# Turning the keys of 13 units in place of 9 with VectorE and GpSimd, and scaling both output halves with one multiply

## The chip, the cores and the metric

The kernel runs on one core of a Trainium2 chip. The metric is device microseconds of one execution, without the host. Each kernel ran several times; medians and ranges are given, and states are compared only among "fast" runs, as all profiled runs here were. Four engines matter: TensorE (PE in the profile; PEld is its weight load), ScalarE (ACT), VectorE (DVE) and GpSimd (POOL). SyncE (SP) issues the DMAs.

## The reference, cut to what matters

```python
B, Sq, D = 8, 32, 1024;  Hq, Hkv, Sk, Dh = 32, 4, 8192, 128
W = min(4096, max(256, Sk // 4))                  # 2048: the last 2048 keys
q = (x @ wq).reshape(B, Sq, Hq, Dh)               # to (B, Hq, Sq, Dh)
k, v = the last W rows of k_cache, v_cache, each of the 4 heads used by 8 query heads
p = softmax(q @ k^T * Dh**-0.5)
out = (p @ v, back to (B, Sq, Hq * Dh)) @ wo
```

There are 32 units, one for each pair of batch entry and key head: 256 queries against 2048 keys. All in bfloat16.

## The kernel before: the parts that matter

The score matmuls of this kernel take K with the 128 features on the partitions, but memory holds keys by rows. So K of each unit is turned, in one of three ways: units 0 to 4 by TensorE transposes, most others by a transposing DMA, and the units listed in `V_T` by VectorE and GpSimd. In the last way VectorE transposes each 32x32 block where it stands, into a second buffer (4 instructions of 0.685 us each, "blocks"), and then 16 copies of 32 partitions each ("moves", 0.672 us each on GpSimd) put the blocks where they belong. The fifth number of a `V_T` entry says how many of the 16 moves GpSimd takes; VectorE takes the others.

```python
V_T = {5: (2, (5, 6, 8, 10), 10, 17, 12),         # load with unit 2, blocks in these slots, moves from slot 10 to 17, 12 moves on GpSimd
       **{u: (u - 4, range(4 * u - 16, 4 * u - 12), 4 * u - 13, 4 * u - 4, 16) for u in (8, 11, 14, 17, 20, 23, 26, 29)}}
...
self.krp = pool("krp", 4)      # raw K, rows as in memory
self.kbp = pool("kbp", 2)      # K with its blocks turned
self.kvt = pool("kvt", 2)      # kTv: K turned by VectorE and GpSimd
...
        def move(k, d):
            ...
            if d >= V_T[ui][4] // 4:
                nc.vector.tensor_copy(out=out, in_=in_)
            else:
                nc.gpsimd.tensor_scalar(out=out, in0=in_, scalar1=1.0, scalar2=1.0, op0=ALU.mult, op1=ALU.mult)
```

The main loop has four slots to a unit, 128 in all, numbered through. In a slot TensorE computes scores (`s_ps`) for 512 keys, ScalarE their exponentials, and TensorE the product with V (`o_ps`) of two slots earlier. V goes through a VectorE copy (`va`), because a column of ones beside it gives the softmax's sums.

```python
        for ui, (b, g) in enumerate(self.units):
            ...
            if ui:
                self.va_copy(ui)                  # VectorE
            for c in range(NCH):                  # 4 slots
                for u in loads.get(ui * NCH + c, []):
                    self.load_unit(u)             # SyncE
                ... s_ps matmuls, exponential ...
                while len(pv_queue) > 2:
                    pv_queue.pop(0)()             # o_ps matmuls of two slots ago; at a unit's last one: finish_unit
                ...
                for p in plan[ui * NCH + c]:      # pieces of q and output projections, blocks, moves
                    p()
```

`finish_unit` takes the reciprocal of the sums, scales the unit's output in two halves and turns it for the output projection. At the very end a value is read from memory: all engines branch on it, over a slow fallback path, to the last piece of the program.

## Time and profile before

| | before |
|---|---|
| time, median of the 4 runs beside the changed kernel | 186.84 us (186.51 to 187.57) |
| span of the profiled run | 184.6 us |
| TensorE busy | 180.7 us, 98% |
| VectorE busy, GpSimd busy | 115.1 us, 95.0 us |
| waits of TensorE after the start-up | two of its weight loads, 0.4 and 0.2 us, both at the very end |

The page of the kernel before: its busy time by engine, its chain of waits by engine, and two of its groups (busy time, mean nanoseconds of one, idle time before).

```profile
span 184.6 us, 5057 instructions
...
PE 180.7 (98%) x2057; PEld 154.0 (83%) x2057; DVE 115.1 (62%) x266; ACT 131.7 (71%) x133; POOL 95.0 (51%) x150
...
PE 93%; DMA 4%; SPq 1%; issue 0%; DVE 0%
...
L261 POOL TENSOR_SCALAR kTv<-kb 32x512 bf16<-32x512 bf16 x140 | 94.1, 672 | 64.9 <-PE s_ps L468 38.3
...
L421 DVE TENSOR_SCALAR o_sb<-o_ps,RL_all 128x128 bf16<-128x128 f32 x64 | 19.5, 347 | 1.1
```

The list of waits, for TensorE's matmuls alone, has only these two lines, both from the start-up (total us, number, longest):

```profile
PE warm_ps L346 <- PEq L641: 0.8, 1, 0.8
PE q_ps L376 <- DMA wq_sb<-in_wq_dram: 0.3, 1, 0.3
```

So TensorE bounds the kernel, and between the start-up and the last 8 us nothing makes it wait.

### The profile page before, as it was taken

The page shows a single profiled execution, that of the slowest core. Times are in us where ns is not written, and L with a number is a line of the kernel's source. Part 1 is how long each engine was busy: PE and PEld are TensorE (multiplying, and loading weights), DVE is VectorE, ACT ScalarE, POOL GpSimd, SP SyncE. Part 2 cuts the span into 40 slices and gives each one's busy share as a digit, 9 for nine tenths or more (in the row PEclk, how much of TensorE's full clock was granted, in tenths as well). Part 3 has the DMA queues.
Part 4 walks back from the last instruction along what each step waited for, and adds up shares of the span by engine and source line. Part 5 has one row for each costly group of instructions (what it writes and reads, how often), then busy time and mean ns, then how long its engine had stood idle before and what let it go on. Part 6 is the DMA issues. An engine that isn't in the chain of part 4 may idle for free.

```text
span 184.6 us, 5057 instructions
## 1 busy us (share of the span) xinstructions
PE 180.7 (98%) x2057; PEld 154.0 (83%) x2057; DVE 115.1 (62%) x266; ACT 131.7 (71%) x133; POOL 95.0 (51%) x150
## 2 busy tenths in 40 slices
PE   8999999999999999999999999999999999999994
PEld 2789999999999999988788899988787888888843
DVE  0119799994586686586468549656754865265363
ACT  2207899787789777787878677887776888888800
POOL 2000007949939959928954990797199379700000
PEclk9999999999999999999999999999999999999999
DMA  5999999999999999999999999999999999993003
GB/s 161 283 390 407 408 396 395 260 182 380 262 355 208 389 250 240 340 321 302 233 396 251 303 378 308 240 249 409 301 301 342 260 275 313 282 269 47 0 30 94
DMA packets 52954, 51.73 MB, mean 280 GB/s; under 512 B 39744, under 2 KB 40256, under 8 KB 52928
## 3 DMA queue, kind: packets, MB, share of 16 engines
q1 hardware_dynamic: 52352, 50.90, 99.0%
q10 hardware_dynamic: 576, 0.49, 0.8%
q8 instruction: 16, 0.26, 0.6%
q14 instruction: 10, 0.08, 0.2%
HBM read 41.42 MB, written 0.52 MB: 227 GB/s over the span
## 4 chain that ended last, share of the span: by engine, by line
PE 93%; DMA 4%; SPq 1%; issue 0%; DVE 0%
PE o_ps L479 31%; PE s_ps L468 30%; PE op_ps L295 15%; PE q_ps L275 11%; DMA wq_sb<-in_wq_dram 4%; PE q_ps L376 2%; PE tp L236 2%; SPq L164 1%; PE kf_ps L369 1%; SPq L320 0%; DVE o_t L305 0%; PE cnt_ps L533 0%
## 5 line engine op out<-in xcount | busy, mean ns | idle before, releaser
L470 ACT ACTIVATE pT<-s_ps 128x1024 bf16<-128x1024 f32 x128 | 128.8, 1025 | 32.5 <-PE s_ps L468 31.5
L261 POOL TENSOR_SCALAR kTv<-kb 32x512 bf16<-32x512 bf16 x140 | 94.1, 672 | 64.9 <-PE s_ps L468 38.3
L479 PEld LDWEIGHTS <-pT 128*128 128x128 bf16 x1024 | 68.5, 98 | 3.1
L468 PEld LDWEIGHTS <-kT 128*128 128x128 bf16 x368 | 34.8, 98 | 10.3
L295 PE MATMUL op_ps<-wo_sb,OT 128*128 128x512 bf16 (+2 forms) x144 | 36.2, 355 | 0.0
L275 PE MATMUL q_ps<-xT,wq_sb 128*128 128x256 bf16 x192 | 28.2, 273 | 0.0
L479 PE MATMUL o_ps<-va_112,pT 128*128 128x129 bf16 x352 | 27.1, 220 | 0.0
L479 PE MATMUL o_ps<-va_113,pT 128*128 128x129 bf16 x352 | 27.0, 220 | 0.0
L479 PE MATMUL o_ps<-va_114,pT 128*128 128x129 bf16 x320 | 24.7, 220 | 0.0
L251 DVE STREAM_TRANSPOSE kb<-k_raw 128x512 bf16<-128x512 bf16 x36 | 23.8, 685 | 1.2 <-DMA k_raw<-in_k_cache_dram 1.2
L416 DVE RECIPROCAL RL_all<-o_ps 128x2 f32<-128x2 f32 x32 | 5.3, 164 | 25.8 <-PE o_ps L479 25.7
L421 DVE TENSOR_SCALAR o_sb<-o_ps,RL_all 128x128 bf16<-128x128 f32 x64 | 19.5, 347 | 1.1
L468 PEld LDWEIGHTS <-kTv 128*128 128x128 bf16 x144 | 13.9, 98 | 5.1
L275 PEld LDWEIGHTS <-wq_sb 128*128 128x128 bf16 x192 | 17.0, 98 | 1.2
L468 PE MATMUL s_ps<-QT_63,kT 128*128 128x256 bf16 x112 | 16.8, 272 | 0.0
L423 DVE STREAM_TRANSPOSE OT<-o_sb 128x256 bf16<-128x256 bf16 x32 | 14.2, 445 | 1.1
L468 PE MATMUL s_ps<-QT_66,kT 128*128 128x256 bf16 x96 | 14.4, 273 | 0.0
L295 PEld LDWEIGHTS <-OT 128*128 128x128 bf16 x144 | 11.4, 98 | 2.3 <-DVE OT L423 0.2
L468 PE MATMUL s_ps<-QT_65,kT 128*128 128x256 bf16 x80 | 12.0, 273 | 0.0
L468 PE MATMUL s_ps<-QT_64,kT 128*128 128x256 bf16 x80 | 12.0, 272 | 0.0
L302 DVE TENSOR_TENSOR oacc<-op_ps,oacc 128x512 f32<-128x512 f32 x8 | 5.5, 682 | 7.4 <-PE op_ps L295 7.4
L410 DVE COPY va_113<-v_sb 128x2048 bf16<-128x2048 bf16 x11 | 9.8, 888 | 0.0
(44 smaller groups left out, 105.6 us busy)
## 6 DMA issues: line engine op xcount, KB each, us to landing
v_sb<-in_v_cache_dram SPq DMA_DIRECT2D x30, 512.0 KB, 7.6
wo_sb<-in_wo_dram SPq DMA_DIRECT2D x16, 512.0 KB, 6.9
wq_sb<-in_wq_dram SPq DMA_DIRECT2D x13, 512.0 KB, 7.5
k_raw<-in_k_cache_dram SPq DMA_DIRECT2D x13, 512.0 KB, 6.4
wq_sb<-in_wq_dram SPq DMA_DIRECT2D x6, 256.0 KB, 6.5
v_sb<-in_v_cache_dram SPq DMA_DIRECT2D x4, 256.0 KB, 4.9
kT<-in_k_cache_dram SPq DMA_TRANSPOSE x36, 7.3
k_raw<-in_k_cache_dram SPq DMA_DIRECT2D x2, 256.0 KB, 7.6
```

Of the source, the lines that this page charges most:

```text
L251: nc.vector.transpose(out=st["kb"][:, sl, :], in_=self.k_raw[ui][:, sl, :])
L261: nc.gpsimd.tensor_scalar(out=out, in0=in_, scalar1=1.0, scalar2=1.0, op0=ALU.mult, op1=ALU.mult)
L275: nc.tensor.matmul(st["ps"][:, 0:self.NQ], lhsT=self.wq_t[g, i][:, c % (DC // 2), hl * P:(hl + 1) * P], rhs=self.xT[:, c, :], start=(c == ...
L295: nc.tensor.matmul(ps[:, 0:w], lhsT=self.OT[:, gq, c, t * P:(t + 1) * P], rhs=self.wo_t[gq][:, c, n0:n0 + w], start=(k == 0), stop=(k == 7))
L302: nc.vector.tensor_tensor(out=acc, in0=ps[:, 0:w], in1=acc, op=ALU.add)
L410: self.nc.vector.tensor_copy(out=self.va[ui % 3][:, :, 0:self.Dh], in_=self.v_sb[ui][:, :, :])
L416: nc.vector.reciprocal(out=rl[:, ui * QT_N:(ui + 1) * QT_N], in_=o_ps[:, :, Dh])
L421: nc.vector.tensor_scalar(out=o_sb[:, qt, :, :], in0=o_ps[:, qt, 0:Dh].rearrange("p (i c) -> p c i", c=4), scalar1=rl[:, ui * QT_N + qt:ui ...
L423: nc.vector.transpose(out=self.OT[:, g * QT_N:(g + 1) * QT_N, :, b * self.Sq:(b + 1) * self.Sq], in_=o_sb[:, :, :, :])
L468: nc.tensor.matmul(s_ps[:, jj, :], lhsT=self.kT[ui][:, c * CJ + jj, :], rhs=q_u, start=True, stop=True)
L470: nc.scalar.activation(out=pT[:, :, :], in_=s_ps[:, :, :], func=ACT.Exp, bias=0.0, scale=self.scale)
L479: nc.tensor.matmul(o_ps[:, qt, 0:self.VW], lhsT=pT[:, jj, qt * P:(qt + 1) * P], rhs=va[:, j, 0:self.VW], start=(j == 0 and qt == 0), stop= ...
```

## The change

The intent: take more units away from the transposing DMA (14 in place of 18 are left to it), pay for it with VectorE and GpSimd, which had room, and win some VectorE time back by scaling both halves of a unit's output in one instruction.

```diff
 V_T = {5: (2, (5, 6, 8, 10), 10, 17, 12),
-       **{u: (u - 4, range(4 * u - 16, 4 * u - 12), 4 * u - 13, 4 * u - 4, 16) for u in (8, 11, 14, 17, 20, 23, 26, 29)}}
+       **{u: (u - 4, range(4 * u - 13, 4 * u - 9), 4 * u - 10, 4 * u - 2, 12) for u in range(7, 30, 2)}}
...
-        for qt in range(QT_N):
-            nc.vector.tensor_scalar(out=o_sb[:, qt, :, :], in0=o_ps[:, qt, 0:Dh].rearrange("p (i c) -> p c i", c=4),
-                                    scalar1=rl[:, ui * QT_N + qt:ui * QT_N + qt + 1], scalar2=None, op0=ALU.mult)
+        nc.vector.tensor_tensor(out=o_sb[:, :, :, :], in0=o_ps[:, :, 0:Dh].rearrange("p q (i c) -> p q c i", c=4),
+                                in1=rl[:, ui * QT_N:(ui + 1) * QT_N].unsqueeze(2).unsqueeze(3).to_broadcast([P, QT_N, 4, 32]), op=ALU.mult)
```

## The prediction

> **What bounds the kernel now.** TensorE. The page gives PE 98% of a 184.6 us span at a granted clock of 0.9 or more in every slice; the windows show no gap from 12 us to 176 us. The list of waits gives PE only 1.1 us of waiting, all in the start. The chain that ended last is 93% PE: o_ps 31%, s_ps 30%, op_ps 15%, q_ps 11%. There 8 o_ps matmuls advance in 0.45 us and 4 s_ps matmuls in 0.46 us throughout: no hidden waiting. Everything else has room: ACT 71%, VectorE 115.1 us (62%), GpSimd 95.0 us (51%). DMA is nearly always busy (share 1.1 and over in the windows) but runs ahead.
>
> **What the change does, from the groups of the trace.**
> - DMA: 18 units' K by DMA transpose become 14, so 36 transposing issues become 28; 4 plain K loads more, same bytes. PE doesn't wait for it: gain about 0.
> - VectorE blocks: 16 more at 685 ns, +11 us.
> - VectorE moves: 52 in place of 4, at 449 ns, +21.6 us.
> - GpSimd moves: 156 in place of 140, at 672 ns, +10.8 us (to about 106 us).
> - Multiply: two ops spanning 0.61 us become one of 256 elements per partition. [...]
> Net VectorE: about +26 us, to 141 us (76%); 85 to 93% where the work falls.
>
> **Contention.** [...] GpSimd moves have a median of 611 ns but a longest of 1167; the same va copy takes 0.65 us or up to 1.12. [...]
>
> **How much is critical.** Almost nothing. By unit pair (8 slots, 9.7 to 11.5 us of PE): VectorE needs 4 blocks 2.5, 4 moves 1.9, 2 va copies 1.7, [...] casts and sums 1 to 1.6, so 9 to 9.8 us. GpSimd needs 12 moves at about 0.74 us start to start, 8.9 us, with ten slots until the scores want them. The in-order VectorE queue will lag 1 to 1.5 us at worst, but a va copy has two slots of slack, PSUM tiles two, o_ps five. So I expect PE still without waits, or a few short ones (tightest: slots 31 to 38, where PE needs only 0.92 us a slot). [...]
>
> **Prediction: 187.0 us, range 186.2 to 188.9.** Faster by over 2%: 0.02; within 2%: 0.88; slower by over 2%: 0.10.
>
> **What would show it.** Right: PE still about 181 us busy with no waits of note; VectorE about 140 us; GpSimd 104 to 110 us; fewer SyncE waits and higher GB/s[...]. Wrong: PE waiting for va copies, kTv moves or PSUM copies; GpSimd moves averaging over 750 ns.
>
> **What would make it wrong.** [...] the multiply slower with a stride-zero operand; K loads blocked behind the four raw buffers early on. No step can give 2%, as PE's work is untouched.

Where a cut is marked, an explanation or a figure is gone that no trace or run of this case shows. VectorE's net came to +26 us, to 141 us; of its terms +11 us and +21.6 us still stand, and the term for the multiply is cut: how long the one instruction takes was not measured when this was written. The kernel after and e3 measure it: 0.424 us. The 9 to 9.8 us of VectorE for a unit pair hold the two finishes (the kernel after has 0.17 + 0.42 + 0.45 us for one). The 187.0 us had counted almost nothing as critical.

## More of the kernel before

In the stretch from 36 to 60 us, the windows show (busy time and number of instructions of PE, PEld, DVE, ACT, POOL):

```profile
36.00:60.00 24.00, 24.00 (x298) 22.46 (x296) 16.94 (x44) 19.63 (x21) 16.96 (x26) 1.00 1.15 280
```

## The result, and the profile after

The changed kernel took 193.06 us (median of 4 runs, 192.38 to 194.03), against 186.84 us of the kernel before: ratio 1.035, with an interval of 1.0299 to 1.0402. A ratio here and below is the mean time of one kernel's fast runs over the mean of the other's in the same rounds, so it is not quite the ratio of the medians. The prediction, 187.0 us with a range up to 188.9, was wrong, and the outcome was one to which it gave a chance of 0.10.

The page of the kernel after, the same parts and the groups that answer to the change. `va` is the copy of V, `kTv` the moves, `kb` the blocks:

```profile
span 190.2 us, 5101 instructions
...
PE 180.1 (95%) x2041; PEld 153.1 (81%) x2057; DVE 145.2 (76%) x298; ACT 131.7 (69%) x133; POOL 105.5 (55%) x166
...
PE 69%; DVE 11%; DMA 7%; issue 4%; POOL 4%; SPq 1%; ACT 1%; DVEq 0%; POOLq 0%; ACTq 0%
...
L261 POOL TENSOR_SCALAR kTv<-kb 32x512 bf16<-32x512 bf16 x156 | 104.5, 670 | 58.8 <-PE tp L236 26.4
...
L251 DVE STREAM_TRANSPOSE kb<-k_raw 128x512 bf16<-128x512 bf16 x52 | 35.4, 696 | 0.7
...
L410 DVE COPY va<-v_sb 128x2048 bf16<-128x2048 bf16 x32 | 31.0, 968 | 0.4
...
L259 DVE COPY kTv<-kb 32x512 bf16<-32x512 bf16 x52 | 21.9, 421 | 1.1
...
L420 DVE TENSOR_TENSOR o_sb<-o_ps,RL_all 128x256 bf16<-128x256 f32 x32 | 13.6, 424 | 1.1
```

TensorE does the same work, but the chain of waits now runs 69% through it and not 93%. The list of waits of the kernel after names what it waits for, on the matmul side (PE) and on the weight side (PEld); the longest wait for kTv shows on both, with 1.5 us on the weight side and 1.3 us on the matmul side:

```profile
PEld L467 <- POOL kTv L261: 2.5, 3, 1.5
...
PEld L478 <- issue: 1.0, 3, 0.4
...
PEld L236 <- DMA k_raw<-in_k_cache_dram: 0.8, 1, 0.8
...
PE s_ps L467 <- ACT pT L469: 0.3, 1, 0.3
PE o_ps L478 <- DVE va L410: 0.2, 1, 0.2
```

The three of "PEld L478" have no releaser of their own there; they are the `o_ps` matmuls that wait for a `va` copy, as the last line says of one of them, and f2 below confirms it for all three. The wait put down to `pT` falls together with that for kTv of unit 29 (slot 116), so it is not an eighth.

Where each is in time can be read by lining up the 128 exponentials of the two traces, which all are recorded, and taking the difference of their starts. It is constant almost everywhere and grows at seven slots. Of the 3.8 us reached at slot 116, 2.1 us come with kTv, 0.9 us with `va` copies and 0.8 us with raw K:

| slot | lag behind the kernel before | what TensorE waited for there |
|---|---|---|
| up to 12 | -0.06 us | |
| 13 | 0.77 us | raw K of unit 4, from the DMA |
| 23 | 1.06 us | `va` copy of unit 5 |
| 36 | 2.48 us | kTv of unit 9 |
| 99 | 2.79 us | a `va` copy |
| 107 | 3.08 us | a `va` copy |
| 108 | 3.34 us | kTv of unit 27 |
| 116 to 127 | 3.80 us | kTv of unit 29 |
| end of the span | 5.6 us | see below |

The last 1.8 us come after the last exponential. The timelines of VectorE behind the branch, first of the kernel before, then of the kernel after, show the idle time before the first instruction there in brackets:

```profile
178.40 0.69 DVE L305 TENSOR_TENSOR o_t<-op_ps,oacc 128x512 bf16<-128x512 f32 x1 [0.24 <-PE op_ps L295]
180.20 1.54 DVE L305 TENSOR_TENSOR o_t<-op_ps,oacc 128x512 bf16<-128x512 f32 x3 [1.10 <-PE op_ps L295]
```

```profile
182.20 0.69 DVE L305 TENSOR_TENSOR o_t<-op_ps,oacc 128x512 bf16<-128x512 f32 x1 [0.43 <-PE op_ps L295]
185.90 1.42 DVE L305 TENSOR_TENSOR o_t<-op_ps,oacc 128x512 bf16<-128x512 f32 x4 [3.00 <-PE op_ps L295]
```

The gap is 3.00 us in place of 1.10. The profile names TensorE as the releaser, but that is only the semaphore that the instruction waits for. The matmul concerned ended at 180.09 us before, and VectorE began 0.11 us later; in the kernel after it ended at 183.89 us, and VectorE began only 2.0 us later. The chain of waits of the kernel after gives the truer name: "issue", which is time in which nothing recorded was waited for (start, length):

```profile
182.90 2.92 issue
```

### The profile page after: what moved, and what is told of

Read it like the earlier page. It is cut to its first block, busy times and chain, and to the rows that moved or that the text cites. A ratio compares the mean times of both kernels' runs of the same rounds, so it can differ in the third digit from the quotient of the medians.

```text
span 190.2 us, 5101 instructions
## 1 busy us (share of the span) xinstructions
PE 180.1 (95%) x2041; PEld 153.1 (81%) x2057; DVE 145.2 (76%) x298; ACT 131.7 (69%) x133; POOL 105.5 (55%) x166
## 4 chain that ended last, share of the span: by engine, by line
PE 69%; DVE 11%; DMA 7%; issue 4%; POOL 4%; SPq 1%; ACT 1%; DVEq 0%; POOLq 0%; ACTq 0%
PE o_ps L478 24%; PE s_ps L467 23%; PE op_ps L295 11%; PE q_ps L275 8%; POOL kTv L261 4%; DMA wq_sb<-in_wq_dram 4%; DVE kb L251 3%; DMA k_raw<-in_k_cache_dram 3%; DVE va L410 3%; DVE kTv L259 2%; PE q_ps L376 2%; PE tp L236 1%; SPq L164 1%; DVE OT L422 1%; DVE o_sb L420 1%
## 5 line engine op out<-in xcount | busy, mean ns | idle before, releaser
L261 POOL TENSOR_SCALAR kTv<-kb 32x512 bf16<-32x512 bf16 x156 | 104.5, 670 | 58.8 <-PE tp L236 26.4
L478 PE MATMUL o_ps<-va,pT 128*128 128x129 bf16 x1024 | 78.8, 220 | 0.5 <-DVE va L410 0.2
L478 PEld LDWEIGHTS <-pT 128*128 128x128 bf16 x1024 | 68.4, 98 | 4.0 <-issue 1.0
L467 PE MATMUL s_ps<-QT,kT 128*128 128x256 bf16 x304 | 45.6, 273 | 0.0
L251 DVE STREAM_TRANSPOSE kb<-k_raw 128x512 bf16<-128x512 bf16 x52 | 35.4, 696 | 0.7
L467 PE MATMUL s_ps<-QT,kTv 128*128 128x256 bf16 x208 | 31.2, 273 | 1.8 <-POOL kTv L261 1.3
L410 DVE COPY va<-v_sb 128x2048 bf16<-128x2048 bf16 x32 | 31.0, 968 | 0.4
L259 DVE COPY kTv<-kb 32x512 bf16<-32x512 bf16 x52 | 21.9, 421 | 1.1
L420 DVE TENSOR_TENSOR o_sb<-o_ps,RL_all 128x256 bf16<-128x256 f32 x32 | 13.6, 424 | 1.1
L416 DVE RECIPROCAL RL_all<-o_ps 128x2 f32<-128x2 f32 x32 | 4.8, 148 | 10.3 <-PE o_ps L478 10.3
L278 DVE CAST QT<-q_ps 128x256 bf16<-128x256 f32 x24 | 9.6, 398 | 3.7 <-PE q_ps L275 3.6
L376 PE MATMUL q_ps<-xT,wq_sb 128*128 128x256 bf16 (+1 forms) x80 | 8.0, 251 | 1.2 <-DMA wq_sb<-in_wq_dram 1.1
```

The costliest lines, as they stand in the source:

```text
L251: nc.vector.transpose(out=st["kb"][:, sl, :], in_=self.k_raw[ui][:, sl, :])
L376: nc.tensor.matmul(qs[h // 2][:, h % 2, n0:n1], lhsT=self.wq_t[0, c // H][:, c % H, h * P:(h + 1) * P], rhs=self.xT[:, c, n0:n1], start=(c ...
L410: self.nc.vector.tensor_copy(out=self.va[ui % 3][:, :, 0:self.Dh], in_=self.v_sb[ui][:, :, :])
L420: nc.vector.tensor_tensor(out=o_sb[:, :, :, :], in0=o_ps[:, :, 0:Dh].rearrange("p q (i c) -> p q c i", c=4), in1=rl[:, ui * QT_N:(ui + 1) ...
L467: nc.tensor.matmul(s_ps[:, jj, :], lhsT=self.kT[ui][:, c * CJ + jj, :], rhs=q_u, start=True, stop=True)
L478: nc.tensor.matmul(o_ps[:, qt, 0:self.VW], lhsT=pT[:, jj, qt * P:(qt + 1) * P], rhs=va[:, j, 0:self.VW], start=(j == 0 and qt == 0), stop= ...
```

## The experiments

There were two theories to be split for the seven waits. **P, placement:** each load or VectorE operation concerned stands a little too late in its queue, and the same work done a little earlier costs nothing. **W, work:** VectorE and GpSimd have too much to do, and a wait taken away in one place comes back in the next. For the end of the kernel: **F:** VectorE's program has grown, so its branch stands at another place in it, and the gap depends on that place. **Q:** it is backlog or TensorE. Twelve kernels ran, and all gave correct results.

### The end: e1, e2, h1

Edit of all three: some memsets of one element per partition in front of VectorE's program, where VectorE is idle (its first instruction of the program starts at 5.55 us in the kernel before, at 5.16 us in the kernel after), so that everything behind them stands that many instructions later. Only the numbers differ: 8 in the kernel after (e1), 37 and 20 in the kernel before (e2, h1).

```diff
+        pad_sb = self.c1.tile([P, 1], BF16, name="pad_sb")
+        for _ in range(8):        # e2: 37, h1: 20, in the kernel before
+            nc.vector.memset(pad_sb[:, :], 0.0)
         nc.sync.dma_start(out=x_sb[:, 0, :], in_=xf[0:P, :])
```

> The kernel after, with 8 one-element-per-partition memsets put at the front of VectorE's program, where VectorE has nothing to do. In the profile after, VectorE's first instruction behind the branch at the end comes 3.0 us after the branch, before it was 1.1 us. Theory F [...]: the gap falls to about 1.1 us and the time by about 1.9 us, to some 191.1 us; the seven waits of TensorE before stay at 3.8 us. Rival Q (the wait is VectorE's own backlog, or TensorE ending later): 8 more instructions change nothing or add a little, 193 us, gap still 3 us.

> The kernel before with 37 such memsets at the front of VectorE's program, so that its branch and target stand at the places that they have in the kernel after. Nothing else changes and no engine is any busier after 10 us. Theory F: the gap behind VectorE's branch grows from 1.1 to about 3.0 us and the time by about 1.9 us, to 188.7 us, with TensorE without a wait up to the branch. Rival Q: the time stays at 186.8 us, as VectorE has no backlog here.

> The kernel before with 20 memsets in front of VectorE's program: branch near instruction 297[...]. Theory F: no longer gap behind the branch (1.1 us), 186.2 to 187.0 us. Rival (any longer VectorE program costs at the branch, in proportion): about 0.8 us more, 187.4 us.

| run | median (range) | ratio to before, interval | gap before VectorE's first instruction behind the branch |
|---|---|---|---|
| e1, after + 8 | 191.38 (191.19 to 191.66) | 1.0258, 1.0225 to 1.0291 | 1.10 us |
| e2, before + 37 | 188.09 (187.7 to 188.38) | 1.0083, 1.0048 to 1.0118 | 3.49 us |
| h1, before + 20 | 188.29 (187.13 to 188.67) | 1.007, 1.0024 to 1.0116 | 3.23 us |

The timeline of VectorE behind the branch, of e1 and then of e2:

```profile
184.26 1.54 DVE L305 TENSOR_TENSOR o_t<-op_ps,oacc 128x512 bf16<-128x512 f32 x3 [1.10 <-PE op_ps L295]
```

```profile
182.42 1.42 DVE L305 TENSOR_TENSOR o_t<-op_ps,oacc 128x512 bf16<-128x512 f32 x4 [3.49 <-PE op_ps L295]
```

More instructions in front of the kernel after take the gap away; more in front of the kernel before bring it. That is what F says and Q cannot say. So that the gap depends on the position is shown; what VectorE does in it is not, as the chain has only "issue" there (2.92 us in the kernel after).

h1 was a miss. I had estimated that with 20 more instructions the gap would stay short; it was 3.23 us. Over all kernels, the gap was 1.10 us where 245, 265, 277, 322, 326 or 346 recorded VectorE instructions stand before the branch, and 3.0 to 3.5 us where there are 297 or 314. So position decides, not length; where between 277 and 297 the gap grows, and where between 314 and 322 it shrinks, is left open.

### The two halves of the change: e3, e4

e3 is the kernel before with the multiply of the change alone; e4 is the kernel after with the two multiplies of before.

> The kernel before with the broadcast multiply alone. Theory: harmless; the multiply takes 0.42 us in place of 0.61 us for two, VectorE about 6 us less busy, no waits of TensorE, time 186.6 to 186.9 us. Rival (the multiply with a stride-zero operand contends or delays o_ps): over 187.5 us.

> The kernel after with the two multiplies of before, so the turning alone. VectorE is some 6 us busier than after. Theory: the loss is all from the turning; TensorE's waits for va copies and kTv moves grow from 3.0 us to 4 to 7 us with the busier VectorE[...]: 191.5 to 195 us. Rival (the multiply is at fault): about 187 us.

e3 took 186.82 us (186.02 to 187.58), ratio 1.0003, interval 0.9957 to 1.0048: the multiply is harmless, and no gain either. Its group of instructions is the same as in the kernel after, 424 ns each. e4 took 192.16 us (192.05 to 194.1), ratio 1.0338, interval 1.0275 to 1.0401, although its gap behind the branch is 1.1 us, with 32 more instructions on VectorE. Up to the last exponential it lags 5.35 us behind the kernel before, where the kernel after lags 3.80 and e1, the same kernel but for the memsets, 4.06. So the loss is the turning's, and the multiply won back part of it: 1.29 to 1.55 us by these profiled executions, 0.8 us by the medians of e4 and e1, neither of which has the gap.

### The seven waits one kind at a time, and together: f1, f2, f3, f4

All four start from e1 (after + 8 memsets), in which the gap behind the branch is 1.10 us; in the four it is 1.1 us too.

f1: unit 7's raw K is loaded with unit 4's loads, no more with unit 3's.

```diff
-       **{u: (u - 4, ..., 12) for u in range(7, 30, 2)}}
+       7: (4, range(15, 19), 18, 26, 12),
+       **{u: (u - 4, ..., 12) for u in range(9, 30, 2)}}
```

> The kernel after with the 8 memsets [...], and unit 7's raw K asked for with unit 4's loads, not ahead of them with unit 3's. Base: 191.4 us, with TensorE's wait in slot 13 for unit 4's raw K at 0.84 to 1.1 us. Theory P (each wait is a matter of order: a load or a VectorE op stands a little too late, and can stand earlier at the same work): that wait goes, the others stay; 190.4 us. Rival W (VectorE and GpSimd simply have too much work, and a wait taken away in one place comes back in the next): 191.4 us.

f2: the `va` copy of unit 5 and of units 8 to 31 is issued one slot earlier.

```diff
-            if ui:
+            if ui and not (ui == 5 or ui >= 8):
                 self.va_copy(ui)
             ...
             for c in range(NCH):
+                if c == NCH - 1 and (ui == 4 or 7 <= ui < len(self.units) - 1):
+                    self.va_copy(ui + 1)
```

> The kernel after with the 8 memsets, and the va copies of unit 5 and of units 8 to 31 issued one slot earlier, ahead of that slot's other VectorE work. Base 191.4 us with three waits of TensorE for va copies (about 0.6, 0.35 and 0.3 us). Theory P: these three go, the waits for kTv (1.5, 0.3, 0.8 us) stay within 0.3 us: 190.2 us. Rival W: the blocks behind the copies come later, kTv waits grow by as much: 191.4 us or more.

f3: blocks and moves of units 9 to 29 stand two slots earlier (unit 7's entry as it was). f4: all three.

```diff
-       **{u: (u - 4, range(4 * u - 13, 4 * u - 9), 4 * u - 10, 4 * u - 2, 12) for u in range(7, 30, 2)}}
+       7: (3, range(15, 19), 18, 26, 12),        # f4: 4 in place of 3
+       **{u: (u - 4, range(4 * u - 15, 4 * u - 11), 4 * u - 12, 4 * u - 4, 12) for u in range(9, 30, 2)}}
```

> The kernel after with the 8 memsets, and blocks and moves of units 9 to 29 two slots earlier. The work is the same. Base 191.4 us with TensorE waiting for kTv 1.5, 0.3 and 0.8 us, of which 2.1 us reach the end. Theory P: these three go, those for va stay or shift a little: 189.3 us. Rival W: VectorE lags as much as before plus something, kTv waits stay over 1.5 us in sum: 190.8 to 191.5 us.

> The three together, with the 8 memsets: unit 7's load later, va copies and turning earlier. VectorE and GpSimd do exactly the work of the kernel after (VectorE about 146 us, GpSimd about 105 us). Theory P: all seven waits go, 186.6 to 187.4 us, as fast as before. Rival W: waits of 2 us and more remain somewhere, 189 us or more.

| run | median (range) | ratio to before, interval | waits of TensorE that are left after the start-up (weight side) |
|---|---|---|---|
| e1 | 191.38 (191.19 to 191.66) | 1.0258, 1.0225 to 1.0291 | all seven |
| f1 | 189.98 (189.44 to 190.18) | 1.0157, 1.008 to 1.0233 | all but unit 4's raw K |
| f2 | 189.9 (189.63 to 190.47) | 1.0168, 1.009 to 1.0245 | raw K 1.2; kTv of unit 9 1.6, of unit 29 1.0; one of 0.2 in slot 32 |
| f3 | 189.94 (189.01 to 190.11) | 1.0151, 1.0071 to 1.0231 | raw K 0.8; `va` 0.3, 0.4, 0.4, 0.2; kTv of unit 7 1.0 |
| f4 | 187.79 (186.76 to 188.44) | 1.0045, 0.996 to 1.0129 | kTv of unit 7 0.6; raw K in slot 5 0.2 |

The medians of e1 and of f1 to f4 are from different rounds, and the intervals of f1 to f3 still reach that of e1, so the traces decide here. In f1 the wait for raw K is gone and the others stayed within 0.3 us, as P says. In f2 the three `va` waits are gone, and the one for kTv of unit 27, but those of units 9 and 29 grew by 0.1 and 0.3 us: a little of W. In f3 the three waits for kTv are gone, but of the 2.1 us expected only 1.4 came: the `va` waits of slots 99 and 107 went too, and four others appeared. Three are for `va` copies, in slots 35, 39 and 106; one is in slot 28, for unit 7's kTv, as the waits of f3 show:

```profile
PEld L482 <- issue: 1.4, 4, 0.4
PEld L471 <- POOL kTv L262: 1.0, 1, 1.0
```

Unit 9's earlier moves had got between the last moves of unit 7 in GpSimd's queue. Together (f4) the three edits leave only that one, and 0.2 us for a raw K; the time, 187.79 us, is a little above the 187.4 that P allowed.

### All waits taken away: g1

Unit 7's last two blocks both go to slot 17, and its moves begin in slot 17, so that unit 9 no longer gets in between. Otherwise g1 is f4.

```diff
-       7: (4, range(15, 19), 18, 26, 12),
+       7: (4, (15, 16, 17, 17), 17, 25, 12),
```

> The kernel with all three orders mended and the 8 memsets, in which one wait was left (0.6 us in slot 28, for unit 7's kTv, because unit 9's earlier moves got between unit 7's). Unit 7's last two blocks now both stand in slot 17 and its moves begin one slot earlier. Theory P: that wait goes, TensorE has none over 0.1 us between 14 us and the end; time 186.2 to 187.2 us, ratio to before 0.998 to 1.003. Rival W: a wait of 0.5 us and more remains or comes elsewhere, ratio 1.004 and over.

g1 took 186.97 us (6 runs, 186.02 to 187.37), ratio 1.0005 to before, interval 0.9968 to 1.0042. These are all its waits on the matmul side, both from the start-up:

```profile
PE warm_ps L350 <- PEq L646: 0.8, 1, 0.8
PE q_ps L380 <- DMA wq_sb<-in_wq_dram: 0.6, 2, 0.4
```

On the weight side only the 0.4 us at the very end is left, which the kernel before has too. VectorE (144.3 us) and GpSimd (105.5 us) are about as busy as in the kernel after (145.2 and 105.5 us). In the stretch from 36 to 60 us, where the kernel after lost most, the windows of the kernel after and then of g1 read:

```profile
36.00:60.00 24.00, 22.58 (x276) 20.77 (x274) 22.63 (x49) 17.99 (x18) 17.10 (x27) 1.00 1.12 297
```

```profile
36.00:60.00 24.00, 24.00 (x296) 22.28 (x295) 22.90 (x49) 19.59 (x21) 19.78 (x30) 1.00 1.13 330
```

VectorE is busy 22.63 of 24 us in the one and 22.90 in the other; TensorE waits in the one and not in the other. Theory W falls: the amount of work fits. What did not fit was its order. W has this much right: with so little idle time left, moving one piece shifted others, as f2 and f3 show.

### The split of the moves: g2, g3

g2 gives GpSimd all 16 moves of each of the 13 units. g3 is the kernel before, 9 units, with 12 of 16 moves on GpSimd (and 16 memsets in front, so that more VectorE instructions stand before the branch than where the gap was long; it was 1.1 us).

> The kernel after with all 16 moves of each of the 13 units on GpSimd, none on VectorE. If VectorE's moves are what costs (theory V), VectorE falls to about 123 us, va copies wait less, and the time falls to about 188 us. If GpSimd could not carry them (theory G): 16 moves at about 0.74 us start to start are 11.8 us, against 9.7 to 11.5 us of TensorE for two units, so every second unit's kTv comes later than the one before, with waits of TensorE of 10 us and more in sum: 196 to 205 us. I expect G: the split is needed for 13 units.

> The kernel before, 9 units, with 12 of 16 moves on GpSimd in all of them, and 16 memsets in front [...]. VectorE gains 32 moves, about 14 us, to about 130 us; GpSimd falls to 108 moves, about 72 us. Theory (it is the sum of 13 units in their places, not the split, that costs): no wait of TensorE over 0.4 us, 186.4 to 187.5 us. Rival (moves on VectorE are harmful by themselves): kTv or va waits of over 1 us, over 188 us.

g2 took 205.99 us (205.63 to 206.31), ratio 1.1042, just above the range expected of G. VectorE fell to 117.7 us and waited more, but GpSimd could not keep up; the list of waits of g2:

```profile
PEld L467 <- POOL kTv L261: 18.3, 10, 3.2
```

So 13 units need VectorE's help. g3 took 186.19 us (185.62 to 186.7), ratio 0.9973, interval 0.9929 to 1.0017: as fast as before, with VectorE at 131.5 us, GpSimd at 73.0 us, and no wait of TensorE but a 0.4 us one for a raw K in slot 5, which e2 (0.3 us) and e3 (0.5 us), equally built on the kernel before, show there too (h1 0.7 us, in slot 3). The moves on VectorE are not harmful by themselves. No version was shown to beat the kernel before; g3's interval contains 1.

## Why the prediction was wrong

**Right: what bounds the kernel, and that the DMA relief wins nothing.** TensorE's own work stayed 180 us, the transposing issues fell from 36 to 28, and g1, which keeps all of this and loses nothing elsewhere, is at 1.0005 of before.

**Right: the multiply.** Measured, the one instruction takes 0.424 us, in place of two that span 0.60 us in the kernel before. It saved 5.9 us of VectorE (group of 19.5 us to 13.6), which is about what the net of +26 us had taken off for it; e3 shows that this alone is worth nothing here.

**Right in kind, mis-sized: VectorE's total.** Predicted 141 us, measured 145.2. The moves (21.9 us for 52) and blocks (35.4 us) came out as costed. What had been left out is that the `va` copies, which did not change, would lengthen: three groups summing to 25.4 us before, 31.0 us after. The two traces show which copies are long. In both traces 6 of the 32 copies overlap no GpSimd move and take 0.68 us on average; the 26 that do take 0.82 us before and 1.04 us after. What differs is which came first. In the kernel after all 26 began while a move ran, and each ended 0.55 us (0.549 to 0.552) after the end of that move; before, 19 did, and the 7 that began ahead of a move took 0.65 us. No run was made to keep the moves apart from the copies, so that the moves lengthen them rests on this sorting alone. The total itself is not what cost the time, as g1 has 144.3 us and loses none.

**Wrong: "a va copy has two slots of slack, PSUM tiles two, o_ps five. So I expect PE still without waits, or a few short ones".** This is the step that failed, together with "ten slots until the scores want them" for GpSimd's 12 moves; TensorE waited seven times in the loop, up to 1.5 us, 3.8 us in all. The slack was counted in slots of the program, as if VectorE came to each slot's pieces when TensorE did, with a lag of 1 to 1.5 us "at worst". Unit 9 shows what was overlooked. Its last block stands in slot 26, whose exponential begins at 47.57 us. The timelines of the kernel after, of VectorE, GpSimd and TensorE:

```profile
49.77 0.69 DVE L251 STREAM_TRANSPOSE kb<-k_raw 128x512 bf16<-128x512 bf16 x1
```

```profile
50.65 8.75 POOL L261 TENSOR_SCALAR kTv<-kb 32x512 bf16<-32x512 bf16 x12 [2.27 <-DVE kb L251]
```

```profile
57.54 0.62 PE L478 MATMUL o_ps<-va,pT 128*128 128x129 bf16 x8
59.45 0.61 PE L467 MATMUL s_ps<-QT,kTv 128*128 128x256 bf16 x4 [1.29 <-POOL kTv L261]
```

VectorE began that block 2.2 us after the exponential of its slot, GpSimd's 12 moves took 8.75 us (8.9 predicted), and TensorE was ready for them at 57.98 us (59.45 less the 1.47 us of the weight load's wait), as it needs only 0.90 us a slot from slot 33 on. The moves had 7.3 us from GpSimd's start at 50.65 us, not ten slots, when already eight had been costed at 9.7 us or more. The prediction had the right duration, named slots 31 to 38 as the tightest, and had the two added up in averages over 8 slots. The `va` half failed in the same way. The copy of unit 24 stands ahead of slot 96, whose exponential began at 139.62 us; VectorE came to it at 141.21 us, 1.6 us later, and took 1.08 us. The `o_ps` matmuls that need it, two slots on, waited 0.36 us. The lag is no single number: the list of waits shows that VectorE stood waiting for TensorE at a unit's end 23 times before (25.7 us in all) and only 9 times after (10.3 us).

**Named as a risk, and not costed: the four buffers of raw K.** The prediction lists "K loads blocked behind the four raw buffers early on" among what could make it wrong. That is the wait of slot 13. In the kernel after, units 2, 5, 3 and 7 take the four buffers, in this order, so unit 4's K, which TensorE turns in slots 12 to 15, is asked for only when unit 2's buffer is free. The list of waits of SyncE, before and after, shows that wait grow:

```profile
SPq L193 <- PE tp L236: 3.1, 1, 3.1
```

```profile
SPq L193 <- PE tp L236: 5.5, 2, 4.4
```

Unit 4's load was issued at 17.6 us before and at 23.3 us after. In the kernel before it was unit 8's K, needed much later, that took the wait. f1 undid it, for 1.4 us (191.38 to 189.98, medians of different rounds; the lag at the last exponential fell from 4.06 to 2.61 us).

**Not seen at all: the gap at the end.** About 1.9 us of the 5.6 us by which the span grew (a gap of 3.00 us in place of 1.10) come with the place of VectorE's branch in its program. e1 and e2 show it from both sides, with 1.7 us off the kernel after (193.06 to 191.38, medians of different rounds) and 1.5 us on the kernel before (186.59 to 188.09, of the same).

In sum: of the 5.6 us, 3.8 us are seven waits in the loop, all removed by reordering, and 1.8 us is the end, removed by eight otherwise useless instructions. The prediction's range failed because it had allowed for slack in averages, and for time only where instructions run.

## What to carry to other kernels

When work is added to an engine that has room on average, compute each deadline from when the engine really reaches the piece and from the shortest slots ahead of it, not from averages over the loop: here the same work, at the same 94% to 95% load of VectorE in one stretch, cost 1.4 us there in one order and nothing in another. A load that is placed earlier can take the buffer of one that is needed sooner. And when a program branches near its end, look at the idle time behind the branch after every change, as a change in the number of instructions can by itself cost time there, here 1.5 us (e2).
